# A fused attention, expert and MLP kernel: order of the attention's step, place of its copies, and time of its word loads

## The chip, the cores and the metric

The kernel runs as one program on one core of a Trainium2 chip. The metric is the device time of one execution in microseconds (us). The engines named here are TensorE (PE; PEld is its weight load), VectorE (DVE), ScalarE (ACT), GpSimd (POOL) and SyncE (SP), whose queue issues nearly all transfers. Each engine works through its own queue in order.

## What is computed

Three layers follow one another. The attention has two batches of 8 heads, 768 positions and 64 features; a query sees only the keys of its own cluster. Then each of the 1536 tokens goes through one of 8 experts, and all of them through an MLP with a softplus.

```python
q_assign = np.argmax(np.einsum('bhsd,hcd->bhsc', q_n, c_n), axis=-1)
k_assign = np.argmax(np.einsum('bhsd,hcd->bhsc', k_n, c_n), axis=-1)
mask = q_assign[:, :, :, None] == k_assign[:, :, None, :]
scores = np.where(mask, scale * np.matmul(q, k.transpose(0, 1, 3, 2)), -1000000000.0)
attn = np.exp(scores - np.max(scores, axis=-1, keepdims=True))
attn = attn / (np.sum(attn, axis=-1, keepdims=True) + 1e-09)
x = np.matmul(attn, v)
...
h = np.maximum(x[mask] @ w1[e], 0.0)
out[mask] = gate_w[mask, None] * (h @ w2[e])
...
h = x @ w_in
g = np.maximum(h, 0.0) + np.log1p(np.exp(-np.abs(h)))
return (g @ w_out).astype(np.float32)
```

## The kernel before

**The attention is a ring of 96 steps.** Step g belongs to head h = g // 6 and to its block t = g % 6 of 128 queries. What a step does stands in the loop near the end of the function `body`, and since the schedule there is written by hand, each engine gets its instructions in the order in which the code calls them:

- `av_step(g)` (AV, L356): one of six products of the head before's transposed probabilities with its values, two matmuls. A head's fifth call does two of them and then `fin_av`: ScalarE copies the sum (xTu, L363) and VectorE forms the reciprocals of the row sums (rec, L367 and L368). The sixth call does nothing. So of a head's six steps four hold one piece of AV, one holds two and one none.
- `S_mm(g + 2)`: the scores of the step after next, four matmuls (L305, L320) into one of two PSUM buffers, and VectorE's row maximum nm (L322). The buffer is free when the exponential of step g has read it.
- `P_T(g)`: six transposes of step g's probabilities (Tp, L344) into two PSUM buffers of three, and the copies of the two into PT in SBUF. The second copy is always ScalarE's (L349); the first is VectorE's (L347) unless g is in the set `busy`.
- `jobs` of this step: loads, cluster products (four matmuls, L189), groups of three transposes (L212, L228, L386, L417), logit products (four matmuls, L406), routing.
- `S_exp(g + 2)`: ScalarE's exponential with its row sum (L331).
- `after` of this step, and a quarter of the preparation of the head two later (`prep_part`, L278 to L287): kA and qA on ScalarE, kB and qA's lower half on VectorE, then DMAs of mask rows (L296).

**The conversion of the last layer's weights runs beside it.** These weights arrive as 64-bit words, 16 chunks of 1 MB. Chunk j has a first step g0 = cvg[j] = 11 + (19 j) // 4, so a new chunk starts every 4.75 steps, from step 11 to step 82. `cv_load` (L439) is a job of step g0 - 4 and puts the load of words[j] on SP's queue. The words share a pool of two buffers, so words[j] needs the buffer of words[j - 2]. `cv_bits` does four parts at the ends of steps g0 to g0 + 3: first an absolute value on ScalarE (cvd, L452), then four operations on VectorE (L454, L455, L460, L464); the last one reads the words for the last time. `cv_store` at the end of g0 + 4 writes the float32 chunk to HBM.

`busy` holds the steps g0 + 1, g0 + 2 and g0 + 3 of all chunks, 48 of the 96.

**Loads of q and k** (`load_raw`, L174 and L175) for a pair of heads p are jobs of step 12 p - 25. They also need an older buffer to be free, which VectorE last reads in the preparation at the end of step 12 p - 24. Within a step the load of q and k is registered ahead of the load of words. SP's queue is in order, so whatever stands behind a load that waits for its buffer waits too.

After the attention come the expert layer (L819, L844) and the MLP (L1497, L1532, L1580).

Of the kernel before, what the change touches and what calls it, by code (L numbers as in the profile page):

```python
# [32 lines left out]
def body(ctx, tc, qT, kT, vP, cen, mod, wg, bias, w1, w2, win, wout, out):  # L33
# [114 lines left out]
    desc = p_1.tile([128, 16], F32, name="desc")  # L148
    mk_a = p_1.tile([128, 1], F32, name="mk_a")
    mk_b = p_1.tile([128, 1], F32, name="mk_b")  # L150
    busy = set()
    raw, vt, sims, spl, mks, PT, P_t, S_t, nm_t, sums, av_t, xTu, rec, xb, lgT = ({} for _ in range(15))

    pend = []
# [1 line left out]
    def drain():  # L156
        while pend:
            for _ in pend.pop(0):
                pass

    def run(f, *a):

        drain()
        x = f(*a)
        if hasattr(x, "__next__"):
            next(x, None)
            pend.append(x)
# [101 lines left out]
    def prep_part(h, i):  # L269

        p, o = h // 2, 64 * (h % 2)
        if i == 0:
            spl[h] = tuple(p_sp.tile([128, S], F32R, tag=n, name=n) for n in ("qA", "kA", "qB", "kB"))
        qA, kA, qB, kB = spl[h]
        q_s, k_s = (r[o:o + 64] for r in raw[p])
        hi, lo = slice(o, o + 64), slice(64 - o, 128 - o)
        if i == 0:
            act.copy(kA[hi], k_s)  # L278
            pool.tensor_scalar(out=kA[lo], in0=k_s, scalar1=1.0, scalar2=1.0, op0=ALU.mult, op1=ALU.mult)
        elif i == 1:  # L280
            dve.tensor_tensor(out=kB[0:64], in0=k_s, in1=kA[hi].bitcast(F32), op=ALU.subtract)
        elif i == 2:
            act.activation(out=qA[hi], in_=q_s, func=AF.Copy, scale=0.125)
            pool.tensor_scalar(out=qB[0:64], in0=q_s, scalar1=0.125, scalar2=1.0, op0=ALU.mult, op1=ALU.mult)
        else:
            dve.scalar_tensor_tensor(
                out=qA[lo], in0=q_s, scalar=0.125, in1=qA[hi].bitcast(F32), op0=ALU.mult, op1=ALU.subtract  # L287
            )

    def put_mask(h):  # L290
        p, i = h // 2, h % 2
        qA, kA, qB, kB = spl[h]
        for j, x in enumerate((qB, kB)):
            for a in range(2):
                o = 64 * j + 32 * a + 16 * i
                sp.dma_start(  # L296
                    out=x[64:80, a * HS:(a + 1) * HS].bitcast(F32), in_=mks[p][o:o + 16].bitcast(F32)
                )

    def S_part(g):  # L300
        h, t = divmod(g, NT)
        qA, kA = spl[h][:2]
        ps = ps_S.tile([128, 2, 512], F32, tag="s", name="S")
        for i in range(2):
            pe.matmul(  # L305
                ps[:, i, :HS], qA[:, t * 128:t * 128 + 128], kA[:, i * HS:(i + 1) * HS], start=True, stop=False
            )
        S_t[g] = ps

    def S_mm(g):  # L310
        if g >= NH * NT:
            return
        if g not in S_t:
            S_part(g)
        h, t = divmod(g, NT)
        qA, kA, qB, kB = spl[h]
        ps = S_t[g]
        ts = slice(t * 128, t * 128 + 128)
        for i in range(2):
            pe.matmul(ps[:, i, :HS], qB[:80, ts], kB[:80, i * HS:(i + 1) * HS], start=False, stop=True)  # L320
        nm_t[g] = p_m.tile([128, 1], F32, tag="nm", name="nm", bufs=4)
        dve.tensor_reduce(out=nm_t[g], in_=ps[:, :, :HS], axis=AX.XY, op=ALU.max, negate=True)  # L322

    def S_exp(g):
        if g >= NH * NT:
            return
        h, t = divmod(g, NT)
        if t == 0:
            sums[h] = p_m.tile([128, NT], F32, tag="sums", name="sums", bufs=3)
        P_t[g] = p_P.tile([128, 2, HS], F32, tag="P", name="P")  # L330
        act.activation(  # L331
            out=P_t[g], in_=S_t.pop(g)[:, :, :HS], func=AF.Exp, bias=nm_t.pop(g), scale=1.0,
            accum_out=sums[h][:, t:t + 1],
        )

    def P_T(g):
        h, t = divmod(g, NT)
        if t == 0:
            PT[h] = p_PT.tile([128, NT, S], F32, tag="PT", name="PT")
        P = P_t.pop(g)  # L340
        for i in range(2):
            ps = ps_T.tile([128, 3, 128], F32, tag="t", name="Tp")
            for j in range(3):
                pe.transpose(ps[:, j, :], P[:, i, j * 128:(j + 1) * 128], ident)  # L344
            dst = PT[h][:, 3 * i:3 * i + 3, t * 128:(t + 1) * 128]
            if i == 0 and g not in busy:
                dve.tensor_copy(dst, ps)  # L347
            else:
                act.copy(dst, ps)  # L349
# [20 lines left out]
    def av_step(g):  # L370

        h, kt = divmod(g - NT - 1, NT)
        if kt == NT - 1:
            return
        AV(h, kt)
        if kt == NT - 2:
            AV(h, NT - 1)
            fin_av(h)
# [566 lines left out]
    with tc.manual_schedule():  # L945
# [54 lines left out]
        def job(g, f, *a):  # L1000
            jobs.setdefault(g, []).append((f, a))
# [17 lines left out]
            job(6 * h + 14, fin_l, h)  # L1019
            job(6 * h + 15, fin_lT, h)  # L1020

        cvg = [11 + (19 * j) // 4 for j in range(16)]
        for j in range(16):
            g0 = cvg[j]
            job(g0 - 4, cv_load, j)
            for k in range(4):
                after.setdefault(g0 + k, []).append((cv_bits, (j, k)))
                if k:
                    busy.add(g0 + k)
            after.setdefault(g0 + 4, []).append((cv_store, (j,)))  # L1030

        e_t = p_1.tile([128, LROWS // 128 * LW], U32, name="empty")
# [59 lines left out]
        put_mask(1)  # L1092
        for g in range(NH * NT):
            h, t = divmod(g, NT)
            if g > NT:
                av_step(g)
            S_mm(g + 2)
            P_T(g)
            for f, a in jobs.get(g, ()):
                if inspect.isgeneratorfunction(f):  # L1100
                    run(f, *a)
                else:
                    f(*a)
            S_exp(g + 2)
            drain()
            for f, a in after.get(g, ()):
                f(*a)
            h2, i2 = divmod(g - 3, NT)
            h2 += 2
            if 2 <= h2 < NH and i2 < 4:  # L1110
                prep_part(h2, i2)
                if i2 == 0 and h2 > 2:
                    put_mask(h2)
            if g == 8:
                put_mask(2)
# [64 lines left out]
        for i in range(1, LF + 1):  # L1180
            k = i - 1
# [13 lines left out]
        for x in seq:  # L1195
            kd, k, w, h = x
# [38 lines left out]
        for n in range(1, end):  # L1235
            kd, k, w, h = seq[n]
# [8 lines left out]
            while ks < len(halves) and at_load.get(halves[ks], end) < n + (n == 1):  # L1245
                k = halves[ks]
# [171 lines left out]
        for n in range(2, end):  # L1418
            kind, i, layer, s = seq[n]
# [153 lines left out]
        for c, y in enumerate((ys[NM - 1][1], ps_A.tile([128, 512], F32, tag="a", name="o"))):  # L1573
            cs = slice(c * 256, c * 256 + 256)
            for kt in range(16):
                gh, gl = gs[NM - 1, kt // 4]
                hi, lo = wts["out", kt // 2]
                a, k = (kt % 4) * 256 + 128, (kt % 2) * 512 + c * 256
# [50 lines left out]
```

## Time and profile before

| | |
|---|---|
| time, median of 3 runs | 746.4 us (745.55 to 747.06) |
| profiled execution | 748.49 us, its span 746.8 us |
| TensorE busy | 703.2 us, 94% of the span |
| VectorE busy | 457.7 us, 61% |
| ScalarE busy | 392.3 us, 53% |
| GpSimd busy | 160.7 us, 22% |
| mean granted TensorE clock | 0.995 of 2.4 GHz |
| attention | to about 290 us of the span |

The shares are means over stages with different limits: ScalarE and VectorE have most of their work in the attention, TensorE is busy nearly everywhere. Busy time of TensorE is modelled from pipelined matmuls, whose rows overlap. A wait is put down to the instruction that released it last.

### The profile page before, as it was taken

Reading aid. Unit: us, or ns where it says so; the run is one execution under the profiler, and the core shown is the slowest. Engines: PE = TensorE matmul, PEld = TensorE weight load, DVE = VectorE, ACT = ScalarE, POOL = GpSimd, SP = SyncE. Lnnn points to the kernel's source line nnn. Section 1 sums busy time; section 2 is a strip of 40 time slices with the busy share of each in tenths; the row PEclk is TensorE's granted clock in tenths of the full one; section 3 lists DMA queues with packets and bytes.
Section 4 is the critical chain, followed back from the end, with each engine's and each line's share of the span. In section 5 each row is a group of like instructions: output and inputs, shape, how many; then the busy total and the mean of one; then the engine's idle time right before and its main releaser. Section 6 shows DMA issues by size and latency. Waiting matters only on the chain. (4 is left out here: it accounts for less than half of the span.)

```text
span 746.8 us, 11746 instructions
## 1 busy us (share of the span) xinstructions
PE 703.2 (94%) x4498; PEld 562.5 (75%) x4498; DVE 457.7 (61%) x668; ACT 392.3 (53%) x635; POOL 160.7 (22%) x172
## 2 busy tenths in 40 slices
PE   4898999899888999999999999989999999999998
PEld 2665665556455655888898878989889899899887
DVE  4898998799799985865747446684423424323220
ACT  3777886787687876344645535542332332322320
POOL 4501120111231203664362431260000000000000
PEclk9999999999999999999999999999999999999999
DMA  4407354534534525769868964301000100000000
GB/s 136 148 17 257 112 208 145 204 135 160 201 123 145 178 104 183 250 227 397 324 228 310 411 216 168 128 1 29 26 18 15 37 7 29 1 1 29 1 29 28
DMA packets 38683, 100.18 MB, mean 134 GB/s; under 512 B 7934, under 2 KB 15486, under 8 KB 36576
## 3 DMA queue, kind: packets, MB, share of 16 engines
q1 hardware_dynamic: 35888, 92.22, 35.3%
q0 software_dynamic: 2592, 6.79, 2.6%
q8 instruction: 36, 0.59, 0.3%
q10 hardware_dynamic: 144, 0.39, 0.2%
q14 instruction: 23, 0.19, 0.1%
HBM read 79.13 MB, written 19.17 MB: 132 GB/s over the span
## 5 line engine op out<-in xcount | busy, mean ns | idle before, releaser
L1508 DVE SCALAR_TENSOR_TENSOR sp<-g,sp 128x1024 f32<-128x1024 f32 x24 | 29.4, 1224 | 149.7 <-ACT sp L1507 149.7
L1497 PE MATMUL g<-xh,wh 128*128 128x256 f32 x384 | 109.1, 284 | 0.0
L1497 PE MATMUL g<-xl,wh 128*128 128x256 f32 x384 | 108.1, 281 | 0.0
L1497 PE MATMUL g<-xh,wl 128*128 128x256 f32 x384 | 108.0, 281 | 0.0
L331 ACT ACTIVATE P<-S,nm 128x768 f32<-128x768 f32 x96 | 87.0, 906 | 38.8 <-DVE nm L322 34.7
L344 PE MATMUL Tp<-ident,P 128*128 128x128 f32 x576 | 84.7, 280 | 15.3 <-ACT PT L349 9.7
L1505 ACT ACTIVATE sp<-g 128x1024 f32<-128x1024 f32 x24 | 24.6, 1027 | 137.5 <-PE g L1497 127.6
L322 DVE TENSOR_REDUCE nm<-S 128x1 f32<-128x768 f32 x96 | 90.7, 946 | 9.1 <-PE S L320 8.7
L344 PEld LDWEIGHTS Tp<-ident,P 128*128 128x128 f32 x576 | 68.0, 142 | 28.5 <-ACT PT L349 15.2
L742 POOL TENSOR_TENSOR wl<-raw,wh 128x1024 fp32r<-128x1024 f32 x22 | 54.2, 2475 | 131.1 <-ACT wh L741 124.1
L356 PE MATMUL av<-PT,v 128*64 128x384 f32 x384 | 78.9, 506 | 0.0
L742 DVE TENSOR_TENSOR wl<-raw,wh 128x1024 fp32r<-128x1024 f32 x50 | 66.1, 1362 | 13.1 <-ACT wh L741 13.1
L741 ACT CAST wh<-raw 128x1024 fp32r<-128x1024 f32 x69 | 69.0, 1050 | 9.8 <-DMA raw<-in_w 7.2
L1497 PEld LDWEIGHTS g<-xl,wh 128*128 128x128 f32 x384 | 73.5, 191 | 0.5
L1497 PEld LDWEIGHTS g<-xh,wh 128*128 128x128 f32 x384 | 73.4, 191 | 0.5
L1497 PEld LDWEIGHTS g<-xh,wl 128*128 128x128 f32 x384 | 73.3, 191 | 0.0
L349 ACT COPY PT<-Tp 128x384 f32<-128x384 f32 x144 | 64.2, 483 | 14.9 <-PE Tp L344 14.1
L1532 PE MATMUL o<-wh,gT 128*128 128x512 f32 x216 | 69.7, 394 | 0.0
L305 PEld LDWEIGHTS S<-kA,qA 128*128 128x128 f32 x192 | 29.9, 195 | 50.2 <-ACT P L331 13.9
L305 PE MATMUL S<-kA,qA 128*128 128x384 f32 x192 | 60.6, 399 | 4.2 <-ACT P L331 3.8
L844 PE MATMUL y<-wh,hT 128*128 128x512 f32 x192 | 63.1, 398 | 0.0
L819 PE MATMUL h<-xh,wh 128*128 128x256 f32 x192 | 55.0, 287 | 0.5 <-DVEq L1350 0.5
(284 smaller groups left out, 1403.9 us busy)
## 6 DMA issues: line engine op xcount, KB each, us to landing
raw<-in_w SPq DMA_DIRECT2D x56, 512.0 KB, 7.5
words<-in_win SPq DMA_DIRECT2D x8, 1024.0 KB, 5.5
w_rows<-cvt SPq DMA_DIRECT2D x16, 512.0 KB, 3.2
words<-in_wout SPq DMA_DIRECT2D x8, 1024.0 KB, 6.5
whole<-in_w SPq DMA_DIRECT2D x16, 512.0 KB, 6.9
raw<-w_rows SPq DMA_DIRECT2D x16, 512.0 KB, 5.0
rawq<-in_qT SPq DMA_DIRECT2D x8, 384.0 KB, 3.6
v<-in_vP SPq DMA_DIRECT2D x8, 384.0 KB, 4.7
```

Of the source, the lines that this page charges most:

```text
L305: pe.matmul(ps[:, i, :HS], qA[:, t * 128:t * 128 + 128], kA[:, i * HS:(i + 1) * HS], start=True, stop=False)
L322: dve.tensor_reduce(out=nm_t[g], in_=ps[:, :, :HS], axis=AX.XY, op=ALU.max, negate=True)
L331: act.activation(out=P_t[g], in_=S_t.pop(g)[:, :, :HS], func=AF.Exp, bias=nm_t.pop(g), scale=1.0, accum_out=sums[h][:, t:t + 1],)
L344: pe.transpose(ps[:, j, :], P[:, i, j * 128:(j + 1) * 128], ident)
L349: act.copy(dst, ps)
L356: pe.matmul(av_t[h][64 * a:64 * a + 64, :], vt[p][:, kt, 64 * i:64 * i + 64], PT[h][:, kt, a * HS:(a + 1) * HS], start=(kt == 0), stop=(kt ...
L741: cp(self.hi, self.raw)
L742: eng.tensor_tensor(out=self.lo, in0=self.raw, in1=self.hi.bitcast(F32), op=ALU.subtract)
L819: pe.matmul(o, a, b[:, kt, :], start=(n == 0 and f % 2 == 0), stop=(n == 11), skip_group_check=True)
L844: pe.matmul(u["y"][j], x, y, start=(kt == 0 and i == 0), stop=(kt == 7 and i == 2))
L1497: pe.matmul(o, a, b[:, kt, :], start=(n == 0 and f % 2 == 0), stop=(n == 11), skip_group_check=True)
L1532: pe.matmul(ys[u][j], x[:, a:a + 128], y, start=(kt == 0 and i == 0), stop=(kt == 15 and i == 2))
```

## The change

Three edits. `busy` is gone; in its place the condition on g lets VectorE copy only in steps before the first chunk's first step (11) and after the last chunk's step g0 + 3 (85), so in steps 11 to 85 ScalarE makes both copies. `cv_load` is a job of step g0 - 6 instead of g0 - 4. In the loop `S_mm(g + 2)` is called ahead of `av_step(g)`.

```diff
--- before.py
+++ after.py
@@ -148,7 +148,7 @@
     desc = p_1.tile([128, 16], F32, name="desc")
     mk_a = p_1.tile([128, 1], F32, name="mk_a")
     mk_b = p_1.tile([128, 1], F32, name="mk_b")
-    busy = set()
+    cvg = [11 + (19 * j) // 4 for j in range(16)]
     raw, vt, sims, spl, mks, PT, P_t, S_t, nm_t, sums, av_t, xTu, rec, xb, lgT = ({} for _ in range(15))
 
     pend = []
@@ -343,7 +343,7 @@
             for j in range(3):
                 pe.transpose(ps[:, j, :], P[:, i, j * 128:(j + 1) * 128], ident)
             dst = PT[h][:, 3 * i:3 * i + 3, t * 128:(t + 1) * 128]
-            if i == 0 and g not in busy:
+            if i == 0 and not cvg[0] <= g <= cvg[-1] + 3:
                 dve.tensor_copy(dst, ps)
             else:
                 act.copy(dst, ps)
@@ -1019,14 +1019,11 @@
             job(6 * h + 14, fin_l, h)
             job(6 * h + 15, fin_lT, h)
 
-        cvg = [11 + (19 * j) // 4 for j in range(16)]
         for j in range(16):
             g0 = cvg[j]
-            job(g0 - 4, cv_load, j)
+            job(g0 - 6, cv_load, j)
             for k in range(4):
                 after.setdefault(g0 + k, []).append((cv_bits, (j, k)))
-                if k:
-                    busy.add(g0 + k)
             after.setdefault(g0 + 4, []).append((cv_store, (j,)))
 
         e_t = p_1.tile([128, LROWS // 128 * LW], U32, name="empty")
@@ -1092,9 +1089,9 @@
         put_mask(1)
         for g in range(NH * NT):
             h, t = divmod(g, NT)
+            S_mm(g + 2)
             if g > NT:
                 av_step(g)
-            S_mm(g + 2)
             P_T(g)
             for f, a in jobs.get(g, ()):
                 if inspect.isgeneratorfunction(f):
```

On TensorE, at a head's end (the step with two pieces of AV, the step with none, the first step of the next head), before:

```order
L356 MATMUL av<-PT,v 64x384 x4
L305 MATMUL S<-kA,qA 128x384 x2
L320 MATMUL S<-kB,qB 128x384 x2
L344 MATMUL Tp<-ident,P 128x128 x6
L305 MATMUL S<-kA,qA 128x384 x2
L320 MATMUL S<-kB,qB 128x384 x2
L344 MATMUL Tp<-ident,P 128x128 x6
L386 MATMUL misc<-ident,xTu 128x128 x3
L356 MATMUL av<-PT,v 64x384 x2
L305 MATMUL S<-kA,qA 128x384 x2
L320 MATMUL S<-kB,qB 128x384 x2
L344 MATMUL Tp<-ident,P 128x128 x6
```

and now:

```order
L305 MATMUL S<-kA,qA 128x384 x2
L320 MATMUL S<-kB,qB 128x384 x2
L356 MATMUL av<-PT,v 64x384 x4
L344 MATMUL Tp<-ident,P 128x128 x6
L305 MATMUL S<-kA,qA 128x384 x2
L320 MATMUL S<-kB,qB 128x384 x2
L344 MATMUL Tp<-ident,P 128x128 x6
L386 MATMUL misc<-ident,xTu 128x128 x3
L305 MATMUL S<-kA,qA 128x384 x2
L320 MATMUL S<-kB,qB 128x384 x2
L356 MATMUL av<-PT,v 64x384 x2
L344 MATMUL Tp<-ident,P 128x128 x6
```

The scores S, which stood behind AV, now stand ahead of it, so that AV lies between S and the transposes Tp; the step without AV is as it was.

On SP's queue, from the mask rows put down ahead of words[1] to the store of the first attention rows (words are the chunks to be converted, rawq and rawk the loads of q and k, qB and kB mask rows, w_rows the converted chunks), before:

```order
L296 DMA qB<-mk 16x384 x2
L296 DMA kB<-mk 16x384 x2
L174 DMA rawq<-in_qT 128x768
L175 DMA rawk<-in_kT 128x768
L439 DMA words<-in_win 128x2048
L470 DMA w_rows<-cvt 128x1024
L296 DMA qB<-mk 16x384 x2
L296 DMA kB<-mk 16x384 x2
L439 DMA words<-in_win 128x2048
L182 DMA v<-in_vP 128x768
L395 DMA x_rows<-xb 128x6x128
```

and now:

```order
L439 DMA words<-in_win 128x2048
L296 DMA qB<-mk 16x384 x2
L296 DMA kB<-mk 16x384 x2
L174 DMA rawq<-in_qT 128x768
L175 DMA rawk<-in_kT 128x768
L439 DMA words<-in_win 128x2048
L470 DMA w_rows<-cvt 128x1024
L296 DMA qB<-mk 16x384 x2
L296 DMA kB<-mk 16x384 x2
L182 DMA v<-in_vP 128x768
L395 DMA x_rows<-xb 128x6x128
```

words[1], the first words row in the piece before, stood behind the loads of rawq and rawk; it now stands ahead of them and of one set of mask rows. words[2] now follows the pair, where words[1] stood.

On VectorE, at the end of the head that holds steps 18 to 23, before:

```order
L281 TENSOR_TENSOR kB<-rawk,kA 64x768
L367 TENSOR_SCALAR rec<-sums 128x6
L368 RECIPROCAL rec<-rec 128x6
L322 TENSOR_REDUCE nm<-S 128x1
L464 SCALAR_TENSOR_TENSOR cvt<-words,cvt 128x1024
L322 TENSOR_REDUCE nm<-S 128x1
L347 COPY PT<-Tp 128x3x128
L388 TENSOR_TENSOR xb<-misc,rec 128x3x2x64
L286 SCALAR_TENSOR_TENSOR qA<-rawq,qA 64x768
L322 TENSOR_REDUCE nm<-S 128x1
L347 COPY PT<-Tp 128x3x128
```

and now:

```order
L281 TENSOR_TENSOR kB<-rawk,kA 64x768
L322 TENSOR_REDUCE nm<-S 128x1
L367 TENSOR_SCALAR rec<-sums 128x6
L368 RECIPROCAL rec<-rec 128x6
L464 SCALAR_TENSOR_TENSOR cvt<-words,cvt 128x1024
L322 TENSOR_REDUCE nm<-S 128x1
L388 TENSOR_TENSOR xb<-misc,rec 128x3x2x64
L286 SCALAR_TENSOR_TENSOR qA<-rawq,qA 64x768
L322 TENSOR_REDUCE nm<-S 128x1
```

The two copies of Tp are gone from the queue (they are ScalarE's), and the row maximum nm of the step stands ahead of the two operations on rec instead of behind them.

## Rows read from the trace of the kernel before

**Rows 1.** Busy by stretch: from:to, length, PE, PEld, DVE, ACT, POOL, clock, DMA, GB/s.

```profile
30.00:270.00 240.00, 219.41 (x1337) 141.92 (x1339) 214.59 (x351) 187.80 (x382) 46.50 (x59) 0.99 0.46 156
550.00:600.00 50.00, 50.00 (x334) 45.50 (x333) 16.46 (x19) 14.94 (x16) 0.00 (x0) 1.00 0.08 27
```

**Rows 2.** TensorE in order of time; start, duration, instruction, and idle time before it.

```profile
31.98 0.60 PE L305 MATMUL S<-kA,qA 128*128 128x384 f32 x2
...
54.30 0.62 PE L305 MATMUL S<-kA,qA 128*128 128x384 f32 x2
56.99 0.62 PE L305 MATMUL S<-kA,qA 128*128 128x384 f32 x2
59.35 0.62 PE L305 MATMUL S<-kA,qA 128*128 128x384 f32 x2
...
63.14 0.62 PE L305 MATMUL S<-kA,qA 128*128 128x384 f32 x2
...
70.59 0.62 PE L305 MATMUL S<-kA,qA 128*128 128x384 f32 x2
71.40 0.82 PE L344 MATMUL Tp<-ident,P 128*128 128x128 f32 x6
72.15 0.87 PE L356 MATMUL av<-PT,v 128*64 128x384 f32 x4
72.95 0.62 PE L305 MATMUL S<-kA,qA 128*128 128x384 f32 x2
...
77.72 0.62 PE L305 MATMUL S<-kA,qA 128*128 128x384 f32 x2
...
80.72 0.62 PE L305 MATMUL S<-kA,qA 128*128 128x384 f32 x2
...
82.11 0.59 PE L305 MATMUL S<-kA,qA 128*128 128x384 f32 x2
85.70 0.62 PE L305 MATMUL S<-kA,qA 128*128 128x384 f32 x2 [0.87 <-ACT P L331]
...
131.40 0.62 PE L305 MATMUL S<-kA,qA 128*128 128x384 f32 x2
...
141.10 0.62 PE L305 MATMUL S<-kA,qA 128*128 128x384 f32 x2
...
202.40 0.62 PE L305 MATMUL S<-kA,qA 128*128 128x384 f32 x2
...
210.94 0.62 PE L305 MATMUL S<-kA,qA 128*128 128x384 f32 x2
...
281.91 0.62 PE L305 MATMUL S<-kA,qA 128*128 128x384 f32 x2
```

**Rows 3.** In order of time: ScalarE's waits for words, SP's queue; granted clock by stretch.

```profile
63.04 1.13 ACT L452 ACTIVATE cvd<-words 128x1024 f32<-128x1024 f32 x1 [2.35 <-DMA words<-in_win]
...
132.67 1.12 ACT L452 ACTIVATE cvd<-words 128x1024 f32<-128x1024 f32 x1 [4.37 <-DMA words<-in_win]
...
203.41 1.12 ACT L452 ACTIVATE cvd<-words 128x1024 f32<-128x1024 f32 x1 [4.07 <-DMA words<-in_wout]
...
54.21 0.34 SPq L174 DMA_DIRECT2D rawq<-in_qT  x1
...
55.06 0.43 SPq L439 DMA_DIRECT2D words<-in_win  x1
...
137.00:139.00 2.00, 2.00 (x10) 1.91 (x9) 1.59 (x3) 2.00 (x6) 0.00 (x0) 0.50 0.00 0
```

**Rows 4.** Groups by line, 30 to 270 us (mean ns, idle before); L347 over all.

```profile
L331 ACT ACTIVATE P<-S,nm 128x768 f32<-128x768 f32 x84 | 76.2, 907 | 29.7 <-DVE nm L322 25.7 <-DVE pm L614 2.7 <-DVE t L614 0.7
L349 ACT COPY PT<-Tp 128x384 f32<-128x384 f32 x133 | 58.9, 483 | 11.0 <-PE Tp L344 10.4
L452 ACT ACTIVATE cvd<-words 128x1024 f32<-128x1024 f32 x16 | 18.3, 1141 | 10.8 <-DMA words<-in_win 6.7 <-DMA words<-in_wout 4.1
...
L347 DVE COPY PT<-Tp x48: 517/546/549, 22.0 to 289.6; 128x384 f32<-128x384 f32 x48
```

## The prediction

> **What bounds the kernel now.** I read the engines' busy time by stretch first, then TensorE's rows in order of time through the attention, then the groups of ScalarE and VectorE there, then who waited for what.
>
> The second half needs little reading: in a stretch of the last layers TensorE is busy for 50.0 of 50 us while VectorE has 16.5 and ScalarE 14.9 us of work [rows 1]. The change touches none of its instructions, so what the attention saves or loses arrives there one for one.
>
> In the attention, from 30 to 270 us, three engines lie close together: TensorE 219.4, VectorE 214.6 and ScalarE 187.8 us busy of 240 [rows 1]. TensorE's busy share does not tell how much it could give back, since its rows overlap. Its starts do. A step starts with the scores S. From S at 70.59 to S at 72.95 is 2.36 us; within it the transposes Tp start 0.81 later, the values' products AV 0.75 after them, and S again 0.80 after that [rows 2]. The step from 56.99 to 59.35 takes the same 2.36, so this is what TensorE needs with nothing in its way. The other kinds, from the same rows: a step with two pieces of AV takes 3.00 (77.72 to 80.72), one with none 1.39 (to 82.11), three extra transposes add 0.33 (54.30 to 56.99 is 2.69), and four small cluster or logit products add 0.79 (59.35 to 63.14 is 3.79, on a 3.00 step).
>
> From the S at 31.98 to the S at 281.91 there are 87 such intervals, 249.9 us. By the program 59 are plain, 14 hold two pieces of AV, 14 none; 29 groups of three transposes and 9 groups of four products are added: 59 x 2.36 + 14 x 3.00 + 14 x 1.39 + 29 x 0.33 + 9 x 0.79 = 217.4 us. So **32.5 us** of this stretch are waits that other engines put on TensorE, and that is all the change can win. Scaled to 240 us, TensorE's own need is 240 x 217.4 / 249.9 = 208.8 us, less than VectorE's 214.6.
>
> The Trainium skill (Perfetto Trace Analysis, Identifying the Most-Contended Engine) says that matmul busy time is no good measure of how far TensorE is from its limit. The trace agrees: by busy time 240 - 219.4 = 20.6 us could be won at most, by starts 32.5; a sum held to the first would cut the fastest rival below to 20.6.
>
> **Where the 32.5 us lie.** ScalarE waits three times for a load of words: 2.35, 4.37 and 4.07 us [rows 3]. TensorE's starts show what each costs. The two intervals behind each hold a step with no AV, a plain step and two groups of transposes, 1.39 + 2.36 + 0.66 = 4.41 us; they took 7.45 (63.14 to 70.59), 9.70 (131.40 to 141.10) and 8.54 (202.40 to 210.94) [rows 2]. The excess is 3.0 + 5.3 + 4.1 = **12.4 us**, more than ScalarE's own 10.8, partly because TensorE came back at half its clock after the longest wait: granted 0.50 from 137 to 139 us, the 1.2 GHz level [rows 3].
>
> The other 20.1 us are spread. Their common form is a head's end, where the short 1.39 us step lets TensorE run up to the exponential: S at 85.70 came 3.59 after the S before, 0.90 over its 2.36 + 0.33 [rows 2]. ScalarE there waits for VectorE's maximum: 25.7 us in 84 exponentials [rows 4]. VectorE is the late one, having 214.6 us of work against TensorE's need of 208.8.
>
> **Words two steps sooner.** The late load of 55.06 us stands on SP's queue behind the load of rawq at 54.21 [rows 3], which waits for VectorE to finish with an old buffer. By the program this happens when a words load falls on the step of a q and k load or the one after: words 1, 6 and 11, the three seen. At g0 - 6 these three stand ahead of the q and k loads. Words 4 and 9 now fall behind such a pair, but six and five steps before their use, at least 5 x 2.36 = 11.8 us. Passing the other way, a words load may hold SP until words j - 2 have been read, at the end of the same step at the latest; behind it stand the stores of converted rows, q and k loads and mask rows with several steps in hand. So I take the waits as gone: -12.4 us, the one bound. The other is what comes back: these are heads like the one at 85.70, with VectorE's conversion over the head's end, and each may show its 0.90, 2.7 in all. I take half, 1.4: **-11 us**.
>
> **Copies.** The kernel before has 48 copies on VectorE at 546 ns [rows 4]. The condition now leaves those of steps 0 to 10 and 86 to 95, 21, so 27 move. VectorE is rid of 27 x 0.546 = 14.7 us, the upper bound of the gain; ScalarE gets 27 x 0.483 = 13.0 us [rows 4], the upper bound of the loss. VectorE then has 199.9 us, ScalarE 200.8, both below TensorE's 208.8, but close. Before, without the words waits, the stretch would be 227.6 us with a busiest engine of 214.6, a ratio of 1.061. With TensorE's 208.8 as the busiest the same ratio gives 221.5: **-6 us**, near the middle of its bounds.
>
> **S first.** The maximum of step g + 2 also comes ahead of the two small reciprocal operations of a head's end on VectorE, which I cost at nothing. The AV pieces are no less work; the order in the ring of steps only turns, but for one thing. ScalarE's queue has the copies of step g ahead of the exponential of g + 2. Count from the start of S. Before, Tp starts at 0.81, the first three transposes are through at about 1.2 (estimated as half of Tp's 0.75 us), two copies of 0.483 end at 2.2, the exponential of 0.907 [rows 4] at 3.1. Now AV stands between, so Tp starts at 1.6, the copies end at 3.0 and the exponential at 3.9. It is needed two steps later, at 4.72, when S of g + 4 wants its bank. ScalarE's room shrinks from 1.6 to 0.8 us. At the step with two pieces of AV the exponential ends 0.64 later, at 4.5, and is wanted at 3.00 + 1.39 = 4.39, so TensorE waits a little. With 0.2 us each in 14 heads: **+3 us**. The bounds are 0 and, with the copies and conversions behind it, the slower rival.
>
> Sum: -11 - 6 + 3 = -14 us. The profiled execution took 748.49 us (span 746.8 and 1.7 around it), so 734.5; it was 2.1 above the median of 746.4, against which the forecast is **732.4 us**.
>
> **Rivals.**
> - *ScalarE takes back what VectorE gives.* For it: ScalarE goes from 187.8 to 200.8 us in a stretch where it loses 0.8 us of room. Against it: 29.7 us of its idle time stands before exponentials [rows 4]. Relief 0, the rest as above: -11 + 3, 738.4.
> - *All three waits fall together.* VectorE was over TensorE's need and is now well under it. Full bounds, 12.4 + 14.7 - 3 = 24, give 722.3. Against it: a burst of conversion with a head's preparation on VectorE still stands over many heads' ends.
> - *Slower: ScalarE's queue becomes the loop.* Place: the exponential behind the later copies. A conversion's first operation, 1.14 us, sits in that queue 16 times [rows 4] and is more than the 0.8 us of room. If neither it nor the moved copies are hidden, 16 x 1.14 + 13.0 + 3 = 34.2 us of new waits stand against 14.7 + 11 won: +8.5, 754.9. It decides once exponentials end more than 4.72 us after their S. Against it: the kernel before has such steps with both copies on ScalarE, and they are not the long ones.
> - *The words do not come sooner.* If SP stands at the words' pair of buffers as long as it stood behind rawq, the three waits stay: -6 + 3, 743.4. Against it: the buffer is free by the end of the step of issue.
>
> **How the numbers follow.** A measurement of this kernel can tell about 0.2% or 1.5 us from no change: 744.9 to 747.9. Forecast 0.54 (727 to 738); ScalarE takes it back 0.20 (735 to 746, 0.03 of it within the bound); all fall 0.11; slower 0.10; words not sooner 0.05 (0.03 within). Faster 0.54 + 0.17 + 0.11 + 0.02 = 0.84, same 0.06, slower 0.10. The range from 722 to 743 leaves out the slower rival, the lower part of the fast one and the upper ends of the others, 0.2.
>
> **What would show it.** Right: no wait of the conversion's first operation for words; no half clock near 137 us; the last S near 268 instead of 281.91; VectorE's share down, ScalarE's up, fewer waits of exponentials for the maximum and more of copies for transposes. The turned order is wrong if S waits for the exponential in far more steps than before, above all right after the short step. The relief is wrong if VectorE's waits fall but the 87 intervals, less 12.4, keep their 237.5 us. The carrying over is wrong if the time from the last S to the end changes.

## The result, and the profile after

The change takes **736.12 us** (median, 735.97 to 736.16), where the kernel before took 746.62 in the same comparison: a ratio of 0.9861, with a 95% interval of 0.9844 to 0.9878. That is 10.5 us faster. The profiled execution took 735.97 us with a span of 734.3, against 748.49 and 746.8 before.

Busy time by stretch of the changed kernel, with the columns of [rows 1]; the second line is the place where TensorE ran at half its clock before [rows 3], the third a place where it does so now:

```profile
30.00:270.00 240.00, 227.46 (x1394) 142.93 (x1393) 211.83 (x336) 204.84 (x423) 47.25 (x63) 0.99 0.51 160
137.00:139.00 2.00, 1.77 (x11) 0.93 (x9) 1.65 (x3) 2.00 (x6) 0.75 (x1) 1.00 1.03 287
206.00:209.00 3.00, 3.00 (x12) 1.84 (x9) 2.93 (x6) 2.13 (x5) 2.83 (x3) 0.50 0.95 305
```

TensorE and ScalarE are denser in the same 240 us, since more steps lie in them and ScalarE makes 30 more copies there (163 against 133 [rows 4]). The clock near 138 us is now 1.00, the 2.4 GHz level. From 206 to 209 us it is 0.50, the 1.2 GHz level, just after TensorE waited 1.77 us for an exponential (the S at 204.79 below).

TensorE in order of time, with the columns of [rows 2]:

```profile
31.59 0.60 PE L305 MATMUL S<-kA,qA 128*128 128x384 f32 x2
...
67.20 0.60 PE L305 MATMUL S<-kA,qA 128*128 128x384 f32 x2
67.64 0.51 PE L320 MATMUL S<-kB,qB 80*128 80x384 f32 x2
68.07 0.87 PE L356 MATMUL av<-PT,v 128*64 128x384 f32 x4
68.87 0.88 PE L344 MATMUL Tp<-ident,P 128*128 128x128 f32 x6
69.50 0.60 PE L305 MATMUL S<-kA,qA 128*128 128x384 f32 x2
...
72.28 0.62 PE L305 MATMUL S<-kA,qA 128*128 128x384 f32 x2 [0.23 <-ACT P L331]
...
79.86 0.60 PE L305 MATMUL S<-kA,qA 128*128 128x384 f32 x2
82.33 0.62 PE L305 MATMUL S<-kA,qA 128*128 128x384 f32 x2 [0.53 <-ACT P L331]
...
204.79 0.62 PE L305 MATMUL S<-kA,qA 128*128 128x384 f32 x2 [1.77 <-ACT P L331]
...
270.00 0.60 PE L305 MATMUL S<-kA,qA 128*128 128x384 f32 x2
```

The 87 intervals from the first of these S to the last now take 270.00 - 31.59 = 238.4 us, 11.5 less than before [rows 2]. Span less the last S is 464.3 us, against 746.8 - 281.91 = 464.9 before: what the attention saved arrived at the end.

ScalarE's groups from 30 to 270 us, and VectorE's copies over all, as in [rows 4]:

```profile
L331 ACT ACTIVATE P<-S,nm 128x768 f32<-128x768 f32 x88 | 80.1, 910 | 20.1 <-DVE nm L322 18.0 <-DVE t L614 1.2 <-DVE pm L614 0.4
L349 ACT COPY PT<-Tp 128x384 f32<-128x384 f32 x163 | 70.7, 484 | 9.9 <-PE Tp L344 9.2
L452 ACT ACTIVATE cvd<-words 128x1024 f32<-128x1024 f32 x16 | 18.4, 1150 | 0.0
...
L347 DVE COPY PT<-Tp x21: 516/549/558, 22.0 to 278.4; 128x384 f32<-128x384 f32 x21
```

The conversion's first operation (L452) no longer waits for words at all: 0.0 us where 10.8 stood. VectorE has 21 copies instead of 48. Exponentials wait for the maximum 18.0 us in 88, before 25.7 in 84. Copies wait for transposes 9.2 us, before 10.4. On SP's queue the load of words that stood behind rawq and cost the first of the three waits is now ahead of it:

```profile
37.80 0.58 SPq L439 DMA_DIRECT2D words<-in_win  x1
...
53.48 0.33 SPq L174 DMA_DIRECT2D rawq<-in_qT  x1
53.85 0.43 SPq L175 DMA_DIRECT2D rawk<-in_kT  x1
58.03 0.33 SPq L439 DMA_DIRECT2D words<-in_win  x1
```

### The profile page after: what moved, and what is told of

Read it like the earlier page. It is cut to its first block, busy times and chain, and to the rows that moved or that the text cites. A ratio compares the mean times of both kernels' runs of the same rounds, so it can differ in the third digit from the quotient of the medians.

```text
span 734.3 us, 11745 instructions
## 1 busy us (share of the span) xinstructions
PE 700.3 (95%) x4498; PEld 556.1 (76%) x4498; DVE 447.0 (61%) x641; ACT 402.6 (55%) x662; POOL 162.8 (22%) x172
## 5 line engine op out<-in xcount | busy, mean ns | idle before, releaser
L344 PEld LDWEIGHTS Tp<-ident,P 128*128 128x128 f32 x576 | 63.9, 143 | 55.4 <-issue 17.3
L344 PE MATMUL Tp<-ident,P 128*128 128x128 f32 x576 | 86.5, 286 | 5.9 <-DVE PT L347 3.2
L349 ACT COPY PT<-Tp 128x384 f32<-128x384 f32 x171 | 74.6, 484 | 14.4 <-PE Tp L344 13.7
L742 DVE TENSOR_TENSOR wl<-raw,wh 128x1024 fp32r<-128x1024 f32 x50 | 66.3, 1363 | 14.3 <-ACT wh L741 14.2
L819 PE MATMUL h<-xl,wh 128*128 128x256 f32 x192 | 53.9, 281 | 0.0
```

Of the source, the lines that this page charges most:

```text
L742: eng.tensor_tensor(out=self.lo, in0=self.raw, in1=self.hi.bitcast(F32), op=ALU.subtract)
L819: pe.matmul(o, a, b[:, kt, :], start=(n == 0 and f % 2 == 0), stop=(n == 11), skip_group_check=True)
```

## Experiments

The three edits were first run alone and in pairs, so that each has four prices. Edits are against the kernel before, where nothing else is said. Spans are those of the profiled executions, the ratios those of the timed runs to the kernel before on the same chip, with 95% intervals.

### Words alone

```diff
-            job(g0 - 4, cv_load, j)
+            job(g0 - 6, cv_load, j)
```

> Only the words load moves to g0 - 6. Theory A (the forecast's terms hold one by one): the three waits for words go, 12.4 us of intervals, 1.4 come back: 746.6 - 11 = 735.6. Theory B (the words did nearly everything in the change; copies and turned order cancel): 735 to 737 as well. Rival C (most of the room of the words waits is taken up by VectorE's lateness at once, and the rest of the gain comes from the copies): 740 or more.

Measured: 736.88 us, ratio 0.9844 [0.9814, 0.9874], span 733.7. ScalarE's conversion waits for nothing:

```profile
L331 ACT ACTIVATE P<-S,nm 128x768 f32<-128x768 f32 x88 | 79.8, 907 | 33.5 <-DVE nm L322 29.6 <-DVE pm L614 2.8 <-DVE t L614 0.7
...
L452 ACT ACTIVATE cvd<-words 128x1024 f32<-128x1024 f32 x16 | 18.3, 1142 | 0.0
```

The 87 intervals take 238.75 us, 11.2 less than before. The six intervals that held the 12.4 us of excess still hold 1.4, as forecast, and exponentials now wait longer for the maximum (29.6 us against 25.7 [rows 4]). This edit alone is worth as much as the whole change.

### Copies alone

```diff
-            if i == 0 and g not in busy:
+            if i == 0 and not 11 <= g <= 85:
```

> Only the copies of steps 11 to 85 all go to ScalarE, words and order as before. Theory A: VectorE relieved, -6: 740.6. Theory B (ScalarE takes back what VectorE gives): within 2 us of 746.6. Rival C: -8 or more, 738.

Measured: 743.74 us, ratio 0.9906 [0.987, 0.9942], span 743.9. The 87 intervals take 246.6 us, 3.3 less. The words' waits are untouched:

```profile
L452 ACT ACTIVATE cvd<-words 128x1024 f32<-128x1024 f32 x16 | 18.4, 1151 | 10.8 <-DMA words<-in_win 6.7 <-DMA words<-in_wout 4.0
```

### S first alone

```diff
+            S_mm(g + 2)
             if g > NT:
                 av_step(g)
-            S_mm(g + 2)
             P_T(g)
```

> Only S ahead of AV. Theory A (ScalarE's exponential comes after later copies): +3, 749.6, with more waits of S for the exponential. Theory B (TensorE's plain step is shorter in the turned order, 2.31 against 2.36 us over 59 plain steps and 0.06 over 14 double ones, 3.8 us, and pays for the later copies): 742 to 746.

Measured: 749.33 us, ratio 1.0009 [0.9984, 1.0034], span 748.1. Alone it can't be told from no change.

### Words and copies, without S first

> The change without S first. Theory A: the change's 736.1 less the 3 us of the turned order: 733. Theory B (the turned order gains a little on TensorE): 737 to 740, later than the change.

Measured: **732.25 us, ratio 0.9772 [0.9743, 0.98]**, span 730.5: faster than the change, whose interval it does not touch. The exponentials and some starts of S in it:

```profile
L331 ACT ACTIVATE P<-S,nm 128x768 f32<-128x768 f32 x90 | 82.0, 911 | 26.9 <-DVE nm L322 23.2 <-DVE pm L614 1.9 <-DVE t L614 1.1
```

```profile
68.35 0.62 PE L305 MATMUL S<-kA,qA 128*128 128x384 f32 x2
...
70.71 0.62 PE L305 MATMUL S<-kA,qA 128*128 128x384 f32 x2
...
73.06 0.62 PE L305 MATMUL S<-kA,qA 128*128 128x384 f32 x2
...
79.81 0.59 PE L305 MATMUL S<-kA,qA 128*128 128x384 f32 x2
83.37 0.62 PE L305 MATMUL S<-kA,qA 128*128 128x384 f32 x2 [0.83 <-ACT P L331]
```

Two things are to be seen. The plain steps from 68.35 take 2.36 and 2.35 us, with no wait; the change has at the same place 2.30 and then 2.78, with S waiting for the exponential. And the head's end still waits: S at 83.37 comes 3.56 after the S before.

### Words with S first, and copies with S first

> The change without the moved copies: words sooner and S first, the first copies of 48 steps on VectorE as before. Theory A: 746.6 - 11 + 3 = 738.6, later than the change by 2.5 or more. Theory B (copies on ScalarE give nothing once words come in time): 733 to 736, not later than the change.

Measured: 739.79 us, ratio 0.9923 [0.9893, 0.9952], span 737.5.

> The change without the sooner words: copies and S first. Theory A: 746.6 - 6 + 3 = 743.6, with three waits of ScalarE for words of 2 to 4.5 us as before. Theory B: 745 to 749, the same three waits.

Measured: 743.75 us, ratio 0.9963 [0.9929, 0.9998], span 745.8. The 87 intervals take 246.0 us, 0.6 less than with copies alone; the longer span lies behind the last S.

With these, each edit's price in span, beside the four sets of the other two:

| edit | other edits out | with the first other | with the second | with both |
|---|---|---|---|---|
| words (others: copies, S first) | -13.1 | -13.4 | -10.6 | -11.5 |
| copies (others: words, S first) | -2.9 | -3.2 | -2.3 | -3.2 |
| S first (others: words, copies) | +1.3 | +3.8 | +1.9 | +3.8 |

Each span is that of one execution, and executions of one kernel differ: copies alone took 737.29 us at a mean granted clock of 0.998 and 745.64 at 0.991. By the medians of the timed runs, which come in part from different chips, words are worth 7.6 to 12.1 us and copies 3.7 to 5.6; S first costs 0.3 alone, 0.0 beside copies, 2.9 beside words and 3.9 beside both. The signs of words and copies hold in either measure. S first has a clear cost only once the words' waits are gone, as would follow if part of it lay in the time in which TensorE stood still for words anyway; no run shows that this is the reason.

### The exponential ahead of the copies

If S first costs because the exponential stands behind later copies on ScalarE, putting it ahead of them should give that back. In the changed kernel (`x1`) and in words and copies (`x2`), with a third buffer for P:

```diff
-    p_P = at_r.enter_context(tc.tile_pool(name="P", bufs=2, side="right"))
+    p_P = at_r.enter_context(tc.tile_pool(name="P", bufs=3, side="right"))
...
+            S_exp(g + 2)
             P_T(g)
...
-            S_exp(g + 2)
```

> The change, with ScalarE's exponential of step g + 2 queued ahead of the two copies of step g instead of behind them (and a third buffer of P, which that order needs). Theory A (S first costs its 4 us because the exponential stands behind copies that come one AV later): the cost goes, span 734.3 to 730 or below, and TensorE's waits of S for the exponential (17.5 us over both rows, 30 to 270 us) fall under half. Rival (the cost is that AV no longer covers TensorE while it waits for the exponential, whoever is late): span stays at 733 or more.

Measured: 754.18 us, ratio 1.0081 [1.0052, 1.011], span 754.3.

> Words and copies without S first (span 730.5), with the same exponential ahead of the copies and the third buffer of P. Theory A: here the copies are through before the maximum is, so the order of the two hardly matters: 729 to 732. Rival (the copies delay the exponential here too): 726 or less.

Measured: 770.45 us, ratio 1.0301 [1.0268, 1.0335], span 768.5.

Both went the other way. The waits of the first from 30 to 270 us (us in all, times, longest):

```profile
PEld Tp L344 <- ACT PT L349: 66.8, 71, 2.4
...
ACT P L331 <- DVE nm L322: 41.3, 34, 3.1
PE Tp L344 <- ACT PT L349: 28.0, 31, 2.1
```

The exponential waits for the maximum, 41.3 us in all, and the copies now wait behind it on ScalarE, so TensorE's transposes wait for copies, where in the change the same two rows are 14.2 and 2.3 us. S itself no longer waits for the exponential, where the change has 17.5 us over both rows of that wait. The edit replaced the cost that it was to measure by a larger one, and tells nothing of S first. It does show that the copies ahead of the exponential are work that ScalarE can do while VectorE is late. What the third buffer does alone was not run.

### S first only at the heads' ends

In words and copies, only for the steps with two pieces of AV, where the prediction had put the cost:

```diff
+            two = g > NT and (g - NT - 1) % NT == NT - 2
+            if two:
+                S_mm(g + 2)
             if g > NT:
                 av_step(g)
-            S_mm(g + 2)
+            if not two:
+                S_mm(g + 2)
```

> Words and copies, with S first only in the 16 steps that hold two pieces of AV. If the cost of S first sits at the heads' ends, as the forecast had it (0.2 us each): span 730.5 + 3 = 733.5. If it sits in the plain steps behind a conversion's or preparation's operation on ScalarE: 730.5 to 731.5.

Measured: 731.58 us, ratio 0.9795 [0.9766, 0.9823], span 729.7, against 730.5 without it; the 87 intervals take 234.55 us against 234.76. In these steps S first costs nothing that can be seen, so its cost is in the others. TensorE's waits for the exponential from 30 to 270 us show it; the change first:

```profile
PEld S L305 <- ACT P L331: 11.3, 22, 2.0
...
PE S L305 <- ACT P L331: 6.2, 16, 1.8
```

and words and copies:

```profile
PEld S L305 <- ACT P L331: 12.5, 18, 1.7
...
PE S L305 <- ACT P L331: 2.8, 4, 1.0
```

The matmuls of S themselves wait 16 times instead of 4. Taken interval by interval against the prediction's own need, the change has 43 that are over 0.1 us too long, words and copies 29.

### S, then the transposes, then AV

In words and copies, S first but with AV behind the transposes, so that the copies come no later against S than before:

```diff
+            S_mm(g + 2)
+            P_T(g)
             if g > NT:
                 av_step(g)
-            S_mm(g + 2)
-            P_T(g)
```

> Words and copies, with the step in the order S, Tp, AV: S is still first, but AV no longer lies between S and the transposes. Theory A (S first costs because the copies, and with them the exponential, come one AV later after S): the cost of 3.8 us goes, span 730 to 732, and the exponential starts about 3.3 us after its S as without S first (3.27 against 3.84 in the change). Rival (whatever stands behind S first, S ahead of AV gives up the cover that AV was for a late exponential): 733 or more.

Measured: 738.29 us, ratio 0.9885 [0.9849, 0.9921], span 736.4. The hoped return to 732 is missed. The 87 intervals take 236.95 us, 1.5 less than the change's; what is lost lies elsewhere. ScalarE waits for the AV of a head's end (6.3 us, against 4.0 in the change), and behind the intervals comes a stretch where the clock falls (1.00 in the change):

```profile
L363 ACT COPY xTu<-av 128x384 f32<-128x384 f32 x14 | 6.8, 484 | 6.3 <-PE av L356 6.3
```

```profile
270.00:280.00 10.00, 7.08 (x35) 3.24 (x35) 5.08 (x10) 4.74 (x9) 0.00 (x0) 0.85 0.39 141
```

So the test brought in costs of its own. By the program, its order from S to S is that of words and copies, only with each piece of AV a step later, and the change has AV later in the same way: ScalarE waits for AV in both, in words and copies only 0.1 us. The exponential starts 3.63 us after its S here (mean of 88 steps), 3.87 in the change and 3.27 in words and copies, so over half of its delay stays with the copies back in their place. How much of S first's price comes from the copies' place, and how much from the later AV, is not settled, nor is the rival named before the run, that S ahead of AV gives up cover for a late exponential.

### The preparation of keys, moved away from the heads' ends

Two tries to shorten VectorE's burst at a head's end, both in words and copies. First the subtraction for kB goes to GpSimd:

```diff
-            dve.tensor_tensor(out=kB[0:64], in0=k_s, in1=kA[hi].bitcast(F32), op=ALU.subtract)
+            pool.tensor_tensor(out=kB[0:64], in0=k_s, in1=kA[hi].bitcast(F32), op=ALU.subtract)
```

> Words and copies without S first, and one operation of each head's preparation (kB, 0.95 us on VectorE just ahead of the late maximum at a head's end) moved to GpSimd. If the waits that remain at the heads' ends are VectorE's burst there, as the forecast says, 13 of these leave the late queue and about half shows: 730.5 - 6 = 724.5. If the relief is hidden like that of the copies (3 us for 14.7): 728 to 731. If GpSimd is then late with kB: above 731.

Measured: 738.43 us, ratio 0.9875 [0.9841, 0.9909], span 737.6, so 7.1 us slower than without it. Of these 3.4 lie in the 87 intervals (238.1 us against 234.76); the rest was not traced, and the mean granted clock is 0.992 here and 1.00 there. Why VectorE won nothing stands under the hardware below.

Then it stays on VectorE but comes four steps later:

```diff
+            if 2 <= h2 < NH and i2 == 5:
+                prep_part(h2, 1)
...
-                prep_part(h2, i2)
+                if i2 != 1:
+                    prep_part(h2, i2)
```

> Words and copies without S first, and the preparation's kB, 0.95 us on VectorE, moved from the fifth step of a head (just ahead of the late maximum) to the third step of the next, still on VectorE; it is first needed two steps later. Theory A (the copies gave 3 us instead of 6 because the waits that are left come from the conversion and the preparation meeting on VectorE at a head's end, where no copy was): 13 or 14 operations leave that queue, half of their 13 us shows: span 730.5 - 6 = 724.5, at least below 728. Rival (the waits there come from ScalarE): 729.5 to 731.5.

Measured: 745.77 us, ratio 0.9969 [0.9941, 0.9998], span 744.2. The head's end did heal:

```profile
80.65 0.59 PE L305 MATMUL S<-kA,qA 128*128 128x384 f32 x2
83.31 0.62 PE L305 MATMUL S<-kA,qA 128*128 128x384 f32 x2
```

2.66 us instead of 3.56, with no wait. Three heads of the 14 healed in this way; in the others the interval behind the short step stayed as long or grew. But the old rawk is now read later, its next load waits on SP's queue for kB (first line), and the cluster products of TensorE wait for the load:

```profile
SPq L175 <- DVE kB L281: 25.5, 5, 5.6
...
PEld misc L189 <- DMA rawk<-in_kT: 9.3, 5, 3.5
...
PE misc L189 <- DMA rawk<-in_kT: 5.8, 5, 2.8
```

The five intervals with these products are 11.4 us over their own need, where words and copies have 0.0. That is the same kind of wait as the words' before the change, made anew at another buffer.

## Why the prediction was right, and where it was not

**The sum.** Forecast 732.4 us by way of -14; measured 736.12 by way of -10.5, inside the range and with the forecast's sign. Against the profiled execution the forecast was 734.5, and 735.97 was measured. Over the 87 intervals the edits gave, one after the other, -11.2 for words, -4.0 for copies and +3.7 for S first, -11.5 in all. Of the 2.5 us that are missing 2 are the copies', the term that was too hopeful. Of the signs named for a right forecast one did not come: copies did not wait more for transposes (9.2 us against 10.4).

**Words, -11.** Right in cause, place and size. Moved alone they gave 11.2 us over the 87 intervals. The method behind it, counting TensorE's lateness from S to S and not ScalarE's own 10.8 us of waiting, gave 12.4 as the bound, and the 1.4 left in these places is the 1.4 taken, which had been set at half of a range. The rival in which the words do not come sooner fell with the 0.0 of L452.

**Copies, -6.** The sign is right, the size too large: 4.0 us of intervals beside the words' edit, 2.3 to 3.2 us of span in single executions, 3.7 to 5.6 by medians. The step that was too hopeful is the ratio: that the stretch would stay 1.061 times its busiest engine's work. It spreads VectorE's relief evenly, and the waits are not even. In words alone the three intervals at a head's end (in the order before, the one without AV and the two behind it; the first of the 87 is left out) hold 15.2 of 20.0 us of excess over own need, and moving the copies took 1.1 us of these, and 2.9 of the other 4.8. The prediction's sign against the relief (the 87 intervals keep 237.5 us) did show in the change, with 238.4; only the single edits tell that the relief came and S first took it back. At the head's end shown here VectorE had no copy to lose. VectorE in words alone, in order of time, ahead of the wait that [rows 2] shows at 85.70:

```profile
78.19 1.21 DVE L460 SCALAR_TENSOR_TENSOR cvt<-words,cvt 128x1024 int32<-128x1024 int32 x1
79.43 0.95 DVE L281 TENSOR_TENSOR kB<-rawk,kA 64x768 fp32r<-64x768 f32 x1
...
80.72 0.92 DVE L322 TENSOR_REDUCE nm<-S 128x1 f32<-128x768 f32 x1
...
83.56 0.55 DVE L347 COPY PT<-Tp 128x384 f32<-128x384 f32 x1
```

The maximum at 80.72 is late behind a conversion operation and the kB subtraction. The first copy comes at 83.56, after the S that was late:

```profile
82.78 0.62 PE L305 MATMUL S<-kA,qA 128*128 128x384 f32 x2 [0.86 <-ACT P L331]
```

Taking copies away leaves that wait as it was: 0.86 us here, 0.83 in words and copies. Taking the subtraction away removes it (2.66 us, above), but in three heads only, so what holds the other heads' ends is not shown. The prediction had named this burst as the reason against the fastest rival, but did not let it weigh on its own term.

**S first, +3.** The size is near, +3.8 of span and 2.5 to 3.7 of intervals beside the words' edit, but by luck, since the place is wrong. The prediction put it at 14 heads' ends, 0.2 us each, because room shrinks most there; S first at just those steps cost nothing. Its sign of a wrong turned order, S waiting for the exponential in far more steps, did show: 16 waits from 30 to 270 us against 3 in the kernel before. Summing the excess over own need, the three intervals at a head's end have 13.8 us in the change and 14.1 in words and copies; the other three of a head have 6.6 and 1.9. Beside words alone it is 16.0 and 15.2, then 7.2 and 4.8. What the step did get right is the direction at ScalarE: from an S to the start of its exponential it takes 3.87 us in the change (mean of 88 steps) and 3.27 without S first, 0.60 more of the 0.8 expected. The thin room of 0.8 us then fails where VectorE's maximum is 0.9 us late, as ahead of the S at 72.28:

```profile
71.23 0.90 ACT L331 ACTIVATE P<-S,nm 128x768 f32<-128x768 f32 x1 [0.92 <-DVE nm L322]
```

That this delay is the whole cause was argued and not shown, since both tests of it (the exponential ahead, S then the transposes) brought costs of their own. Some 3.2 us of the 6.6 lie in two steps from 200.47 to 208.36 us, where routing work stands on VectorE too. In the first S waits 1.77 us for the exponential; in the second TensorE's clock is down to 0.50 (Result). Words and copies keep 1.00 at that place:

```profile
206.00:209.00 3.00, 3.00 (x20) 1.85 (x19) 2.97 (x5) 2.92 (x7) 1.17 (x1) 1.00 0.43 162
```

So part of S first's price in this execution is the clock. Words with S first shows no such loss there, so that part belongs to how the edits meet, and why was not tried.

One small gain was not forecast: a plain step without waits takes 2.30 us in the turned order (67.20 to 69.50) instead of 2.36. The excess above is counted against 2.36, so it shows S first's waits somewhat too small.

**Slower rival.** ScalarE's queue did not become the loop, though the rival's condition was met. In the change an exponential ends 4.78 us after its S on average, and 42 of 88 end more than 4.72 after it; so do 35 in the kernel before and 23 in words and copies. So this condition does not tell whether the rival holds. What speaks against it is ScalarE's own time: 204.84 us busy of 240, and 20.1 us of idle time ahead of exponentials, 18.0 of it for VectorE's maximum.

**Carrying over.** Right for the change: the time from the last S to the end is 464.3 us, 464.9 before, and 463.4 in words alone and in words and copies. It is not fixed, though: 468.6 in copies with S first, 468.0 in S, transposes, AV.

**The better version.** Words and copies without S first, 0.9772 of the kernel before, beats both kernels. With S first at heads' ends only it is 0.9795, the same within the intervals.

## What to carry to other kernels

Price a wait by how late the bottleneck engine's own starts become, place by place, and price relief in the same way: work taken off a busy engine counts only where it stands ahead of something late, so look for it in that engine's rows just before each long interval. Before an operation is delayed to clear a burst, look at which buffer it reads last, since the next load into that buffer moves with it. And run a bundle's edits singly: here one of three was a loss that the sum hid.

## What the runs showed of the hardware that was not expected

**A small VectorE operation held up by GpSimd.** With the kB subtraction on GpSimd, VectorE's addition of 1e-9 to 128x6 sums (L367) grew. VectorE's groups from 30 to 270 us, words and copies first:

```profile
L367 DVE TENSOR_SCALAR rec<-sums 128x6 f32<-128x6 f32 x14 | 2.3, 165 | 0.2
```

and with the subtraction on GpSimd:

```profile
L367 DVE TENSOR_SCALAR rec<-sums 128x6 f32<-128x6 f32 x14 | 12.5, 893 | 0.0
```

Two places of that run, GpSimd in order of time:

```profile
64.90 2.33 POOL L281 TENSOR_TENSOR kB<-rawk,kA 64x768 fp32r<-64x768 f32 x1 [3.12 <-ACT kA L278]
...
82.27 1.81 POOL L284 TENSOR_SCALAR qB<-rawq 64x768 fp32r<-64x768 f32 x1
```

and VectorE:

```profile
65.46 1.80 DVE L367 TENSOR_SCALAR rec<-sums 128x6 f32<-128x6 f32 x1
...
81.04 2.34 DVE L460 SCALAR_TENSOR_TENSOR cvt<-words,cvt 128x1024 int32<-128x1024 int32 x1
83.31 0.80 DVE L367 TENSOR_SCALAR rec<-sums 128x6 f32<-128x6 f32 x1
```

GpSimd's instructions end at 67.23 and 84.08, VectorE's at 67.26 and 84.11. In the 11 of 14 cases that are stretched to 0.46 us or more, L367 ends 0.02 to 0.03 us after the GpSimd instruction beside it, and L460, 1.21 us elsewhere, takes 2.34 in two places where GpSimd was already at work. Removing 13.3 us of kB from VectorE thus gave 10.2 back at L367 alone, and VectorE's busy time from 30 to 270 us stayed (216.26 us against 215.85). The Trainium skill (SBUF — State Buffer, SBUF: two separate sides) says that the two engines share one pair of ports, for which a VectorE operation contends when it runs in a two-port mode, or has two SBUF inputs while GpSimd's operation reads SBUF; the first to start holds the pair for its whole instruction and the other blocks. The trace agrees in these rows; in which mode L367 ran no run shows.

**A queue serves in order, whatever waits.** The price of moving an operation on ScalarE came out far from its own length: the exponential of 0.91 us put ahead of two copies cost 20.0 us of span in one kernel (734.3 to 754.3) and 38.0 in the other (730.5 to 768.5), since each of its waits for VectorE was passed on to the copies behind it. Part of the 38.0 goes with TensorE's granted clock, whose mean fell from 1.000 to 0.981.
